# First tiles of a fused attention, MoE and MLP kernel: step 0's decays loaded as 8 rows, clipped there and spread over the partitions by products, C and x loaded straight into cleared blocks

## The chip, the cores and the metric

The kernel runs on one core of one Trainium2 chip. The metric is device time in microseconds (us), the median of several runs. Engines: PE is TensorE (PEld its weight loads), DVE VectorE, ACT ScalarE, POOL GpSimd, SP SyncE, whose queue issues most DMA transfers. PSUM is the memory that TensorE writes, SBUF the memory on which the other engines work, both of 128 partitions.

## The reference, cut to what matters

```python
# 1. chunked linear attention with decay: batch 4, heads 8, seq 768, head_dim 32, d_state 16
log_a = np.log(np.clip(a, 1e-06, 1.0))
...
    cum = np.cumsum(la, axis=-1)
    L = np.exp(cum[:, :, :, None] - cum[:, :, None, :]) * causal
    M = np.einsum('bhin,bhjn->bhij', Cc, Bc) * L
    y_intra = np.einsum('bhij,bhjd->bhid', M, xc)
    y_inter = np.einsum('bhin,bhnd->bhid', Cc, state) * np.exp(cum)[:, :, :, None]
    ...
    state = decay_full[:, :, None, None] * state + np.sum(Bx, axis=2)
# 2. top-1 MoE on the 3072 rows of 256: 8 experts, 256 -> 1024 -> 256
xn = x / (np.linalg.norm(x, axis=-1, keepdims=True) + 1e-06)
logits = xn @ en.T / tau
expert_idx = np.argmax(logits, axis=1)
    ...
    h = np.maximum(x[mask] @ w1[e], 0.0)
    out[mask] = gate_w[mask, None] * (h @ w2[e])
# 3. second MLP: 256 -> 2048 -> 256
h = x @ w_in
out = (h * np.cos(h)) @ w_out
```

The decays `a` are clipped to [1e-6, 1]. The products of decays that make up `L` are made here by a scan along a row, with no logarithm.

## The kernel before, in words

Three stages follow each other in one program: the attention with the router, the experts, the second MLP. The order of the instructions on each engine is the order in which the program emits them (`tc.manual_schedule()`). The first tiles of the attention are emitted after a list, the string `g.HEAD`; each of its words is a letter for an operation and a number (the dictionary `start`): `p` pre, `s` scores, `a` and `b` the two parts of `halves`, `y` mid, `e` a piece of `prep`, `i` pieces of `blocks`, `k` some products on zeros that only keep TensorE busy (`keep_warm`, tile `pw`), `l` step_1, `t` pieces of `constants`.

The attention goes in 6 steps t of 128 positions; a step has 4 tiles (t,b), one for each batch b. The partitions of a tile hold a pair (half of heads, position in a chunk of 64) or (head, d_state), so a decay row of one head has to stand on 64 or on 16 partitions. Of a tile these instructions matter here (lines of before):

- `pre`: the scan L171, `L <- ac, DD` on VectorE: `ac` are the decays, the same 2048 numbers on 64 partitions, with a zero at the start of each chunk, and `DD` is 1 where a new row begins; then `last` (L176, VectorE) and `bp <- bn, last` (L178, POOL).
- `scores`: `ps <- CB, BTb` (L189, PE). `CB` holds C in four blocks of partitions, zero elsewhere; `BTb` is B masked by ACT (L147).
- `halves`: `pu <- XB, bp` (L205, PE), `M <- ps, L` (L208, VectorE), the state `st` (L219, L221, VectorE). `XB` holds x in blocks, made by ACT (L152) from `xc`.
- `mid`: `py <- CP, st` (L234) and `py <- M, XB` (L239, both PE), `yT <- py` (L242, ACT).
- once in a step, `prep`: the scan `ee <- az, D` (L158) and four products `CP <- CB, ee` (L161), all VectorE. `az` are the decays again, on 16 partitions for each head.

For steps 1 to 5 the decays are clipped once, all together, as tiles `ao` (L402), stored to DRAM as `acd` and `azd` (L403), and loaded from there, one row on 64 or 16 partitions (`load_ac`, L77; `load_az`, L85). Step 1's loads are issued in `step_1`, behind the stores. Step 0's decays are loaded unclipped from the input with the same spreading transfer (`ac`, four pieces of 128 KB and two of 256 KB, and `azr`, 256 KB) and clipped on 128 partitions by VectorE (`clip_ac` L91, `clip_az` L96). Step 0's `CB` is made from `ct` by masked copies on VectorE (L485) and ACT (L483); the `XB` of steps 0 and 1 is made by ACT. From step 2 on, x is loaded straight into `XB`; C is so from step 1 on.

`experts` (three POOL instructions on `er`, L347 to L351) and `constants` prepare the router: `em` (L408, scaled embeddings, VectorE), its transposition `pe` (PE), `IE` (the identity beside it), `tri`, `acc`, `ident`.

Of the kernel before, what the change touches and what calls it, by code (L numbers as in the profile page):

```python
# [25 lines left out]
C_D, C_EI, C_M4, C_M2, C_ONE, C_ID, C_TRI, C_W = 0, 64, 72, 76, 80, 96, 224, 352  # L26


def consts():
# [12 lines left out]

def attn_router(ctx, tc, g):
# [34 lines left out]

    def load_az(t):
        az = sb2.tile([128, 520], F32, tag="az", name="az")  # L80
        if t == 0:
            T[0]["azr"] = sb2.tile([128, 8, 64], F32, tag="M", name="azr", bufs=3)
            nc.sync.dma_start(T[0]["azr"].rearrange("p c i -> p (c i)"), g.A2[t].unsqueeze(1).to_broadcast([8, 16, 512]))
        else:
            nc.sync.dma_start(az, g.azd[t].unsqueeze(1).to_broadcast([8, 16, 520]))  # L85
# [2 lines left out]
    def clip_ac(c0, c1):

        ac = T[0]["ac"][:, c0:c1]  # L90
        nc.vector.tensor_scalar(ac, ac, 1.0, 1e-6, op0=ALU.min, op1=ALU.max)  # L91
        nc.vector.memset(ac.rearrange("p (q i) -> p q i", i=64)[:, :, 0:1], 0.0)

    def clip_az():
        az = T[0]["az"].rearrange("p (c i) -> p c i", i=65)
        nc.vector.tensor_scalar(az[:, :, 1:], T[0]["azr"], 1.0, 1e-6, op0=ALU.min, op1=ALU.max)  # L96
        nc.vector.memset(az[:, :, 0:1], 0.0)
# [26 lines left out]
    def load_b3(t):  # L124
        if t:
            return
        ct = big.tile([128, 512], F32, name="ct")
        nc.sync.dma_start(ct, g.CT[t])
        T.setdefault(t, {}).update(ct=ct)

    def load_b(t):
# [35 lines left out]
    def pre(t, b):  # L167
# [310 lines left out]
    pre(*tiles[0])
    def masked_c(c0, c1, on_act):
        for p in range(4):  # L480
            o, i, m = CB[0][:, p, c0:c1], T[0]["ct"][:, c0:c1], cst[:, C_M4 + p:C_M4 + p + 1]
            if on_act:
                nc.scalar.activation(o, i, AF.Copy, scale=m)  # L483
            else:
                nc.vector.tensor_scalar(o, i, m, None, op0=ALU.mult)  # L485

    masked_c(0, 128, False)
# [1 line left out]
    for _ in range(4):
        next(first)  # L490
    masked_c(128, 256, False)
    for _ in experts_:
        pass
    first_prep = prep(0)

    def step_1(_):
        store_a()
        nc.sync.dma_start(cst[:, C_ID:], g.CST[:, C_ID:])
        loads = dict(n=lambda: load_b2(1), c=lambda: load_b3(1), a=lambda: load_ac(1, 0, 512), A=lambda: load_ac(1, 512), f=lambda: load_ac(1), z=lambda: load_az(1))
        for op in g.LD:  # L500
            loads[op]()
# [6 lines left out]
    def front_b(n):  # L508
        for _ in fronts[n]:
# [943 lines left out]
```

## Time and profile before

| | |
|---|---|
| median of 3 runs | 578.29 us (577.97 to 578.92) |
| profiled execution | 580.77 us |
| span of its trace, first to last instruction | 579.1 us |
| mean granted TensorE clock | 0.983 of full |
| busy: PE, DVE, ACT, POOL | 95%, 77%, 51%, 54% of the span |

The span is the time from the first to the last instruction of the profiled execution; 1.67 us of its time lie outside the span. All instruction times below come from that one execution.

### The profile page before, as it was taken

The numbers are of one execution on the slowest core, as the hardware profiler recorded it, in microseconds if no ns is written. First come the engines' busy times: TensorE is split into PE (matmuls) and PEld (weight loads), VectorE is DVE, ScalarE is ACT, GpSimd is POOL, SyncE is SP. The second block draws the span as 40 slices with busy tenths as digits, with TensorE's granted clock in tenths as the row PEclk, the third lists the DMA queues.
The fourth block names the chain that finished last, engine by engine and source line by source line (L and its number), as shares of the span: only waits on it lengthen the run. The fifth ranks groups of instructions, "written<-read, shape, count | busy, mean of one in ns | idle before, by whom it ended". The sixth has DMA issues, their size and how long they took to land.

```text
span 579.1 us, 11037 instructions
## 1 busy us (share of the span) xinstructions
PE 552.6 (95%) x4000; PEld 502.0 (87%) x4000; DVE 444.9 (77%) x878; ACT 298.0 (51%) x637; POOL 310.5 (54%) x343
## 2 busy tenths in 40 slices
PE   7899999999798999999999999999999999999994
PEld 5678887898687999998998999999999999999994
DVE  6899999866576998798849867777766777776882
ACT  5253533544356575666756545445445445445562
POOL 4323543462254666474655747746746745745763
PEclk8989999999888999999999999999999999999999
DMA  7999885137675676644210000100100100100000
GB/s 211 243 222 210 198 241 168 41 118 235 199 184 210 183 198 220 222 139 173 82 2 1 2 1 2 36 1 2 37 0 1 38 1 1 38 1 6 33 20 19
DMA packets 28993, 57.00 MB, mean 98 GB/s; under 512 B 7216, under 2 KB 16056, under 8 KB 28184
## 3 DMA queue, kind: packets, MB, share of 16 engines
q1 hardware_dynamic: 26184, 47.77, 29.3%
q0 software_dynamic: 2752, 8.51, 4.3%
q8 instruction: 32, 0.52, 0.4%
q14 instruction: 25, 0.20, 0.1%
HBM read 48.50 MB, written 11.07 MB: 103 GB/s over the span
## 4 chain that ended last, share of the span: by engine, by line
PE 57%; DVE 9%; DMA 4%; issue 2%; ACT 2%; POOL 1%; POOLq 0%; SPq 0%; ACTq 0%
PE po L1372 22%; PE pu L1338 22%; PE py L1204 6%; PE ph L1234 6%; DMA xg<-xs 4%; DVE hl L1239 2%; DVE ta L1090 2%; DVE xg L863 1%; POOL gl L1409 1%; DVE ta L1094 1%; ACT hh L1238 1%; DVE lg L844 1%; DVE lg L840 1%; DVE ta L1088 1%; DVE wof L1101 1%
## 5 line engine op out<-in xcount | busy, mean ns | idle before, releaser
L1409 POOL TENSOR_TENSOR gl<-gg,gh 128x512 fp32r<-128x512 f32 (+1 forms) x111 | 125.7, 1138 | 105.2 <-PE pu L1338 63.4
L1399 ACT ACTIVATE cc<-ff,half 128x512 f32<-128x512 f32 (+1 forms) x112 | 74.2, 663 | 128.9 <-DVE ff L1397 128.9
L1395 DVE TENSOR_SCALAR tt<-pu 128x512 f32<-128x512 f32 (+1 forms) x110 | 67.5, 613 | 64.4 <-PE pu L1338 64.2
L1372 PE MATMUL po<-h,gl 128*128 128x256 f32 x384 | 108.3, 282 | 0.0
L1372 PE MATMUL po<-l,gh 128*128 128x256 f32 x384 | 108.3, 282 | 0.0
L1372 PE MATMUL po<-h,gh 128*128 128x256 f32 x382 | 107.7, 282 | 0.0
L752 POOL TENSOR_TENSOR l<-r,h 128x512 fp32r<-128x512 f32 x50 | 69.5, 1406 | 48.7 <-ACT h L743 48.3
L1372 PEld LDWEIGHTS po<-h,gh 128*128 128x128 f32 x382 | 72.3, 189 | 3.6
L1372 PEld LDWEIGHTS po<-l,gh 128*128 128x128 f32 x384 | 72.6, 189 | 3.1
L1372 PEld LDWEIGHTS po<-h,gl 128*128 128x128 f32 x384 | 73.1, 190 | 0.1
L1397 DVE SCALAR_TENSOR_TENSOR ff<-tt,pu 128x512 f32<-128x512 f32 (+1 forms) x110 | 67.1, 610 | 3.8
L1338 PE MATMUL pu<-yh,il 128*128 128x512 f32 (+1 forms) x192 | 68.6, 357 | 0.0
L1338 PE MATMUL pu<-yh,ih 128*128 128x512 f32 (+1 forms) x192 | 68.3, 356 | 0.0
L1338 PE MATMUL pu<-yl,ih 128*128 128x512 f32 (+1 forms) x192 | 68.0, 354 | 0.0
L1405 DVE SCALAR_TENSOR_TENSOR gg<-pu,cc 128x512 f32<-128x512 f32 (+1 forms) x110 | 66.7, 606 | 0.7 <-ACT cc L1399 0.4
L1408 ACT CAST gh<-gg 128x512 fp32r<-128x512 f32 (+1 forms) x112 | 60.8, 543 | 0.7 <-DVE gg L1405 0.6
L1239 DVE SCALAR_TENSOR_TENSOR hl<-ph,hh 128x432 fp32r<-128x432 f32 (+1 forms) x64 | 36.6, 576 | 20.1 <-ACT hh L1238 20.1
L1204 PE MATMUL py<-hl,h 128*128 128x432 f32 (+1 forms) x128 | 46.5, 363 | 4.4 <-DVE hl L1239 4.3
L1238 ACT ACTIVATE hh<-ph 128x432 fp32r<-128x432 f32 (+1 forms) x64 | 32.9, 514 | 28.9 <-PE ph L1234 28.4
L1204 PE MATMUL py<-hh,h 128*128 128x432 f32 (+1 forms) x128 | 46.0, 359 | 1.8 <-ACT hh L1238 1.8
L1204 PE MATMUL py<-hh,l 128*128 128x432 f32 (+1 forms) x128 | 45.9, 359 | 0.0
L1234 PE MATMUL ph<-xl,h 128*128 128x432 f32 x112 | 41.0, 366 | 2.1 <-DVE xl L1057 2.1
(220 smaller groups left out, 1208.4 us busy)
## 6 DMA issues: line engine op xcount, KB each, us to landing
r<-in_w SPq DMA_DIRECT2D x32, 512.0 KB, 5.9
ac<-acd SPq DMA_DIRECT2D x10, 512.0 KB, 6.4
raw<-in_w_in SPq DMA_DIRECT2D x8, 512.0 KB, 6.0
raw<-in_w_out SPq DMA_DIRECT2D x8, 512.0 KB, 3.3
xg<-xs SPq DMA_DIRECT2D x7, 462.4 KB
xs<-zd SPq DMA_DIRECT2D x5, 462.4 KB
XB<-in_X SPq DMA_DIRECT2D x8, 256.0 KB
bt<-in_BT SPq DMA_DIRECT2D x6, 256.0 KB, 8.7
```

Source lines behind the costliest of these rows:

```text
L752: (nc.vector if engines[q] == "v" else nc.gpsimd).tensor_tensor(out=l[:, s], in0=W[e][rn][:, s], in1=h[:, s].bitcast(F32), op=ALU.subtract)
L1204: nc.tensor.matmul(py[m][:, :b_.shape[1]], lhsT=a_[:, q, 128 * m:128 * m + 128], rhs=b_, start=q == 0 and k == 0, stop=q == 7 and k == 2)
L1234: nc.tensor.matmul(ph[:, :n], lhsT=a_[:, c, 128 * f:128 * f + 128], rhs=b_[:, c], start=k == 0, stop=k == 5)
L1239: nc.vector.scalar_tensor_tensor(out=hl, in0=ph[:, :n], scalar=0.0, in1=hh.bitcast(F32), op0=ALU.max, op1=ALU.subtract)
L1338: nc.tensor.matmul(PU[u], lhsT=a_[:, c, 128 * f:128 * f + 128], rhs=b_[:, c], start=c == 0 and k == 0, stop=c == 1 and k == 2)
L1372: nc.tensor.matmul(po[:, i], lhsT=a_[:, s], rhs=b_, start=first and per == 1, stop=q == NF - 1 and k == 2 and i == per - 1)
L1395: nc.vector.tensor_scalar(tt, pu, 0.25, MAGIC, op0=ALU.add, op1=ALU.add)
L1397: nc.vector.scalar_tensor_tensor(out=ff, in0=tt, scalar=-MAGIC, in1=pu, op0=ALU.add, op1=ALU.subtract)
L1399: nc.scalar.activation(cc, ff, AF.Sin, bias=half, scale=-TWO_PI)
L1405: nc.vector.scalar_tensor_tensor(out=gg, in0=pu, scalar=TWO_PI, in1=cc, op0=ALU.mult, op1=ALU.mult)
L1408: nc.scalar.copy(gh, gg)
L1409: (nc.vector if u >= len(units) else nc.gpsimd).tensor_tensor(out=gl, in0=gg, in1=gh.bitcast(F32), op=ALU.subtract)
```

## The change

For step 0 the two inputs of decays are loaded as 8 rows of 512 numbers each (tile `rows`), clipped there by VectorE (`clip_first`, two instructions on 8 partitions), and spread over 128 partitions by f32 products on TensorE with a matrix of ones and zeros (`sel`, 20 KB more of the constants) into PSUM (`spread`): first b = 0 and `az` together, then b = 1 and 2, then b = 3. The scan of b = 0 reads its decays in PSUM; ACT copies the others to `ac` and `az`. The PSUM tile is of the tag `y`, of which there is one buffer, that of `py`. C of step 0 and x of step 1 are loaded straight into `CB[0]` and `XB[1]`, which POOL clears first; `CB[1]` is cleared by VectorE in place of POOL. `DD` and part of `IE` are copied by ACT; the clips of `ao`, the copies of `tri`, `acc` and the rest of `IE` go to POOL. The loads of `em` and `tau` go from POOL's queue to SP's, the square of `em` and `experts` into `constants`, and the words of `g.HEAD` are new.

```diff
+    def load_first():
+
+        T[0] = dict(ac=sb2.tile([128, 2048], F32, tag="ac", name="ac"), az=sb2.tile([128, 520], F32, tag="az", name="az"))
+        a1, a2 = T[0]["rows"] = [sb2.tile([128, 512], F32, tag="M", name="rows", bufs=3)[:8] for _ in range(2)]
+        nc.sync.dma_start(a1, g.A1[0].rearrange("h (b q) -> (h b) q", b=4))
+        nc.sync.dma_start(a2, g.A2[0])
+
+    def clip_first(k):
+        a = T[0]["rows"][k]
+        nc.vector.tensor_scalar(a, a, 1.0, 1e-6, op0=ALU.min, op1=ALU.max)
+        if k == 0:
+            nc.vector.memset(a.rearrange("p (q i) -> p q i", i=64)[:, :, 0:1], 0.0)
+
+    def spread(k):
+
+        o = psY.tile([128, 2, 512], F32, tag="y", name="spread")
+        a1, a2 = T[0]["rows"]
+        ac = T[0]["ac"]
+        for i, b in enumerate(((0, None), (1, 2), (3,))[k]):
+            sel_ = sel[:, :128] if b is None else sel[:, 128 + 128 * b:256 + 128 * b]
+            nc.tensor.matmul(o[:, i], lhsT=sel_, rhs=a2 if b is None else a1, start=True, stop=True)
+        for i, b in enumerate(((0, None), (1, 2), (3,))[k]):
+            if b is None:
+                az = T[0]["az"].rearrange("p (c i) -> p c i", i=65)
+                yield
+                nc.scalar.copy(az[:, :, 1:], o[:, i].rearrange("p (c i) -> p c i", i=64))
+            elif b:
+                nc.scalar.copy(ac[:, 512 * b:512 * b + 512], o[:, i])
+            else:
+                T[0]["ac0"] = o[:, i]
...
-        for p in range(4 if t else 0):
+        for p in range(4):
             nc.sync.dma_start(CB[s][32 * p:32 * p + 32, p], g.CT[t, 32 * p:32 * p + 32])
...
-        if t < 2:
-            xc = T[t]["xc"] = sb2.tile([128, 1024], F32, tag="xc", name="xc")
+        if t < 1:
+            xc = T[t]["xc"] = big.tile([128, 1024], F32, tag="xc", name="xc")
...
-    nc.gpsimd.dma_start(em, g.emb)
-    nc.gpsimd.dma_start(tau, g.tau.unsqueeze(0).to_broadcast([E, 1]))
+    nc.gpsimd.memset(CB[0], 0.0)
+    nc.gpsimd.memset(XB[1], 0.0)
+    nc.vector.memset(warm, 0.0)
...
-    load_az(0)
-    load_ac(0, 512, 1024)
-    load_ac(0, 1024, 2048)
-    nc.gpsimd.memset(CB[1], 0.0)
+    nc.sync.dma_start(em, g.emb)
+    nc.sync.dma_start(tau, g.tau.unsqueeze(0).to_broadcast([E, 1]))
+    nc.sync.dma_start(cst[:, C_ID:], g.CST[:, C_ID:C_W])
+    nc.vector.memset(CB[1], 0.0)
...
     def store_a():
         for k, dst in enumerate((g.acd_t, g.azd_t)):
-            nc.vector.tensor_scalar(ao[k][:, :, 1:], ai[k][:, :, 1 - k:], 1.0, 1e-6, op0=ALU.min, op1=ALU.max)
+            nc.gpsimd.tensor_scalar(ao[k][:, :, 1:], ai[k][:, :, 1 - k:], 1.0, 1e-6, op0=ALU.min, op1=ALU.max)
             nc.sync.dma_start(dst, ao[k])
 
     def constants():
 
+        nc.scalar.activation(e2, em, AF.Square, accum_out=en)
+        for _ in experts():
+            pass
+        yield
         nc.vector.reciprocal(tau, tau)
         nc.vector.tensor_scalar(em, em, er, tau, op0=ALU.mult, op1=ALU.mult)
...
+        nc.gpsimd.tensor_copy(IE[:, :, 0:128], cst[:, C_ID:C_ID + 128].unsqueeze(1).to_broadcast([128, 2, 128]))
+        yield
+        nc.scalar.copy(IE[:, :, 128:], pe)
...
-    g.WARM = 12
-    g.LD = "cnfz"
-    g.HEAD = "k2 l0 i1 a0 z0 m0 c1 k2 z1 s1 k3 b0 p1 k6 i1 s2 e0 c2 k2 k1 i9 a1 b1 y0 e0 p2 e0 e0 t1 k6 t1 t1 t1 t1"
+    g.WARM = 8
+    g.HEAD = "v0 c0 c1 d0 B0 k1 i2 B0 p0 s0 e0 i2 B1 s1 k3 i1 a0 p1 l0 e0 b0 B2 k1 i1 s2 a1 e0 b1 y0 p2 e0 e0 i2 t1 t1 t1 t1 t1 t1"
```

VectorE from its first copy to the first product M of step 0, before (a row is line, operation, out<-in, shape):

```order
L475 COPY DD<-cst 128x512
L91 TENSOR_SCALAR ac<-ac 128x512
L92 MEMSET ac 128x8
L171 SCALAR_TENSOR_TENSOR L<-ac,DD 128x512
L176 TENSOR_TENSOR last<-L,cst 128x16
L485 TENSOR_SCALAR CB<-ct,cst 128x128 x8
L402 TENSOR_SCALAR ao_130<-ai_132 128x3x63
L402 TENSOR_SCALAR ao_131<-ai_133 128x3x64
L208 TENSOR_TENSOR M<-ps,L 128x512
L96 TENSOR_SCALAR az<-azr 128x8x64
```

The same stretch of VectorE in the changed kernel (L184 is the scan, L171 that of `ee`, L221 is M):

```order
L391 MEMSET CB 128x2048
L515 MEMSET az 128x8
L98 TENSOR_SCALAR rows<-rows 8x512
L100 MEMSET rows 8x8
L98 TENSOR_SCALAR rows<-rows 8x512
L184 SCALAR_TENSOR_TENSOR L<-spread,DD 128x512
L189 TENSOR_TENSOR last<-L,cst 128x16
L171 SCALAR_TENSOR_TENSOR ee<-az,D_134 128x520
L221 TENSOR_TENSOR M<-ps,L 128x512
```

The copy of DD, the eight masked copies of C and the two wide clips of `ao` are gone from VectorE; the scan of the first tile stands behind a clear of `CB[1]` and two clips on 8 partitions. From the first scan of step 1 on, VectorE's rows are the same in both programs, in the same order.

ACT before, from the square of `em` to step 1's first block:

```order
L397 ACTIVATE e_200,en<-em 8x256
L147 ACTIVATE BTb<-bt,cst 128x64x2 x2
L147 ACTIVATE BTb<-bt,cst 128x64x6 x2
L152 ACTIVATE XB<-xc,cst 128x32x8 x2
L483 ACTIVATE CB<-ct,cst 128x256 x4
L152 ACTIVATE XB<-xc,cst 128x32x8 x6
L242 COPY yT<-py 128x2x2x64
L147 ACTIVATE BTb<-bt,cst 128x512 x2
```

ACT in the changed kernel, over the same stretch (L114 and L116 copy the spread decays, L165 makes `XB`, L419 is the square of `em`):

```order
L497 COPY DD<-cst 128x512
L160 ACTIVATE BTb<-bt,cst 128x64x2 x2
L114 COPY az<-spread 128x8x64
L160 ACTIVATE BTb<-bt,cst 128x64x6 x2
L116 COPY ac<-spread 128x512 x2
L165 ACTIVATE XB<-xc,cst 128x32x8 x2
L116 COPY ac<-spread 128x512
L165 ACTIVATE XB<-xc,cst 128x32x8 x2
L255 COPY yT<-py 128x2x2x64
L165 ACTIVATE XB<-xc,cst 128x32x8 x4
L419 ACTIVATE e_195,en<-em 8x256
L432 COPY IE<-pe 128x2x8
```

Before, the square of `em` was ACT's first piece of work and all of step 0's `XB` stood ahead of the first `yT`; now four copies of PSUM stand between the blocks, and the square stands behind the last `XB`.

POOL before, from its first `bp` to the fourth:

```order
L178 TENSOR_TENSOR bp<-bn,last 128x256
L347 TENSOR_TENSOR er<-en,pw 8x1
L349 TENSOR_SCALAR er<-er 8x1
L351 TENSOR_TENSOR er<-er,pw 8x1
L178 TENSOR_TENSOR bp<-bn,last 128x256 x2
L807 MEMSET zrow 108x1096
L810 DMA xs<-zrow 64x1096 x2
L178 TENSOR_TENSOR bp<-bn,last 128x256
```

POOL in the changed kernel, from the clips of `ao`, behind the second `bp`, to the fourth `bp` (L191 is `bp`, L360 to L364 `er`, L414 the clips of `ao`):

```order
L414 TENSOR_SCALAR ao_130<-ai_132 128x3x63
L414 TENSOR_SCALAR ao_131<-ai_133 128x3x64
L191 TENSOR_TENSOR bp<-bn,last 128x256
L360 TENSOR_TENSOR er<-en,pw 8x1
L362 TENSOR_SCALAR er<-er 8x1
L364 TENSOR_TENSOR er<-er,pw 8x1
L430 COPY IE<-cst 128x2x128
L434 CAST tri<-cst 128x128
L435 TENSOR_SCALAR acc_127<-cst 128x8
L808 MEMSET zrow 108x1096
L811 DMA xs<-zrow 64x1096 x2
L191 TENSOR_TENSOR bp<-bn,last 128x256
```

Before, `er` stood between the first and the second `bp`, and the clear of `zrow` right behind the third; now the clips of `ao`, on which the stores of the decays wait, stand between the second and the third `bp`, and `er`, the copies and the zeros between the third and the fourth.

## Rows read from the trace of the kernel before

**Rows 1.** The page's first part: busy time of the engines in us, share of the span, instructions.

```profile
PE 552.6 (95%) x4000; PEld 502.0 (87%) x4000; DVE 444.9 (77%) x878; ACT 298.0 (51%) x637; POOL 310.5 (54%) x343
```

**Rows 2.** Busy time in two stretches of the span: the stretch and its length, then PE, PEld, DVE, ACT, POOL busy us (instructions), granted clock, DMA share, GB/s.

```profile
32.00:108.00 76.00, 73.05 (x863) 61.21 (x864) 72.40 (x188) 32.45 (x104) 31.57 (x49) 0.98 0.75 192
...
200.00:579.00 379.00, 369.41 (x2337) 342.92 (x2336) 280.50 (x468) 203.12 (x387) 223.88 (x217) 1.00 0.16 50
```

**Rows 3.** VectorE's waits from 0 to 30 us: waiting instruction, what it waited for, us in total, times, longest.

```profile
DVE DD L475 <- DMA cst<-in_CST: 1.4, 1, 1.4
DVE ac L91 <- DMA ac<-in_A: 1.3, 2, 1.0
...
DVE L L171 <- DMA ac<-acd: 0.9, 1, 0.9
...
DVE az L96 <- DMA azr<-in_A: 0.7, 1, 0.7
```

**Rows 4.** Timeline of VectorE from the scaling of `em` to the second scan of step 1: start us, us, engine, line, operation, tiles; in brackets the idle time ahead and what ended it.

```profile
23.93 0.40 DVE L408 TENSOR_SCALAR em<-em,er,tau 8x256 f32<-8x256 f32 x1
...
25.09 1.15 DVE L171 TENSOR_TENSOR_SCAN L<-ac,DD 128x512 f32<-128x512 f32 x1
...
28.45 1.23 DVE L171 TENSOR_TENSOR_SCAN L<-ac,DD 128x512 f32<-128x512 f32 x1 [0.88 <-DMA ac<-acd]
...
30.24 1.67 DVE L171 TENSOR_TENSOR_SCAN L<-ac,DD 128x512 f32<-128x512 f32 x1 [0.28 <-issue]
```

**Rows 5.** Timeline of VectorE and POOL at the start.

```profile
1.03 0.27 DVE L378 MEMSET warm<- 128x256 uint32 x1
...
2.72 2.30 DVE L475 COPY DD<-cst 128x512 f32<-128x512 f32 x1 [1.40 <-DMA cst<-in_CST]
2.91 1.82 POOL L375 MEMSET CB<- 128x2048 f32 x1
...
6.02 0.43 DVE L91 TENSOR_SCALAR ac<-ac 128x512 f32<-128x512 f32 x1 [1.00 <-DMA ac<-in_A]
...
6.62 1.23 DVE L171 TENSOR_TENSOR_SCAN L<-ac,DD 128x512 f32<-128x512 f32 x1
```

**Rows 6.** TensorE's products in the timeline.

```profile
1.35 5.86 PE L384 MATMUL pw<-warm 128*128 128x272 bf16 x28 [1.35 <-DVE ao L394]
...
9.46 1.98 PE L189 MATMUL ps<-CB,BTb 128*128 128x256 f32 x4 [2.25 <-DVE CB L485]
...
14.06 2.25 PE L384 MATMUL pw<-warm 128*128 128x272 bf16 x18
...
16.14 1.22 PE L189 MATMUL ps<-CB,BTb 128*128 128x256 f32 x4
...
18.35 0.91 PE L205 MATMUL pu<-XB,bp 128*32 128x64 f32 x16 [0.29 <-POOL bp L178]
...
19.18 0.44 PE L234 MATMUL py<-CP,st 128*64 128x128 f32 x4
...
19.45 1.09 PE L239 MATMUL py<-M,XB 128*64 128x64 f32 x16
```

**Rows 7.** TensorE in three windows: the window and its length, PE busy us (instructions), granted clock, DMA share, GB/s.

```profile
10.00:11.00 1.00, 1.00 (x4) 0.50 1.01 274
14.00:15.00 1.00, 1.00 (x10) 1.00 1.04 164
22.00:24.50 2.50, 0.15 (x3) 1.00 1.01 223
```

**Rows 8.** ACT in the timeline, and from the list of groups by form one copy of PSUM later in the program (busy us, mean ns).

```profile
4.48 0.41 ACT L397 ACTIVATE e<-em 8x256 f32<-8x256 f32 x1 [2.12 <-DMA em<-in_emb]
...
4.81 0.18 ACT L397 ACTIVATION_READ_ACCUMULATOR e<-em 8x1 f32 x1
...
9.48 0.91 ACT L152 ACTIVATE XB<-xc,cst 128x256 f32<-128x256 f32 x2 [0.89 <-DMA xc<-in_X]
...
11.90 2.51 ACT L152 ACTIVATE XB<-xc,cst 128x256 f32<-128x256 f32 x6
...
20.59 0.37 ACT L242 COPY yT<-py 128x256 f32<-128x256 f32 x1 [6.18 <-PE py L239]
...
L1029 ACT COPY yd<-py 128x512 f32<-128x512 f32 x1 | 0.6, 592 | 0.0
```

**Rows 9.** POOL in the timeline: the first and the last of the three instructions on `er`, and two `bp`.

```profile
9.00 0.58 POOL L347 TENSOR_TENSOR er<-en,pw 8x1 f32<-8x1 f32 x1
...
10.22 0.57 POOL L351 TENSOR_TENSOR er<-er,pw 8x1 f32<-8x1 f32 x1
...
26.62 0.72 POOL L178 TENSOR_TENSOR bp<-bn,last 128x256 f32<-128x256 f32 x1 [0.92 <-DVE last L176]
...
30.10 0.73 POOL L178 TENSOR_TENSOR bp<-bn,last 128x256 f32<-128x256 f32 x1 [2.33 <-PE py L234]
```

**Rows 10.** SP's issues in the timeline, and the transfers of step 1's and step 2's decays (transfers, KB each, median us from issue to landing, from 0 to 32 us).

```profile
13.70 0.37 SPq L403 DMA_DIRECT2D acd<-ao  x1
...
18.10 1.10 SPq L77 DMA_DIRECT2D ac<-acd  x2
...
ac<-acd SPq DMA_DIRECT2D x4, 512.0 KB, 6.2
...
acd<-ao SPq DMA_DIRECT2D x1, 96.0 KB, 4.3
```

More of the change, by code (lines that the diff above doesn't have):

```diff
@@ L26 @@
 C_D, C_EI, C_M4, C_M2, C_ONE, C_ID, C_TRI, C_W = 0, 64, 72, 76, 80, 96, 224, 352
+C_SEL, C_ALL = 352, 992
 def consts():
-    c = np.zeros((128, C_W), np.float32)
+    c = np.zeros((128, C_ALL), np.float32)
     p = np.arange(128)
+    for k in range(8):
+        c[k, C_SEL:C_SEL + 128] = p // 16 == k
+        for b in range(4):
+            c[k, C_SEL + 128 + 128 * b:C_SEL + 256 + 128 * b] = (p // 64 == k // 4) * (k % 4 == b)
     c[:, C_ID:C_ID + 128] = np.eye(128)
@@ L70, in load_ac @@
     def load_ac(t, c0=0, c1=2048):
-        src = g.A1 if t == 0 else g.acd
+        src = g.acd
         if c0 == 0:
@@ L80, in load_az @@
         az = sb2.tile([128, 520], F32, tag="az", name="az")
[L81 to L85, printed above, removed]
-        T.setdefault(t, {})["az"] = az
[L88 to L97, printed above, removed]
+        nc.sync.dma_start(az, g.azd[t].unsqueeze(1).to_broadcast([8, 16, 520]))
+        T.setdefault(t, {})["az"] = az
+    def load_first():
[3 more added lines that the diff above has]
+        nc.sync.dma_start(a2, g.A2[0])
@@ L122, in load_b2 @@
             nc.sync.dma_start(XB[s][64 * h2:64 * h2 + 64, h2], g.X[t, 64 * h2:64 * h2 + 64])
[L124 to L129, printed above, removed]
     def load_b(t):
@@ L135, in load_b @@
         load_b2(t)
-        load_b3(t)
     def blocks(t):
@@ L148, in blocks @@
                 yield
-        for q in range(4 if t < 2 else 0):
+        for q in range(4 if t < 1 else 0):
             for h in range(2):
@@ L170, in pre @@
         L = sb2.tile([128, 2, 4, 64], F32, tag="L", name="L", bufs=4)
-        nc.vector.tensor_tensor_scan(out=L.rearrange("p c q i -> p (c q i)"), data0=T[t]["ac"][:, 512 * b:512 * b + 512], data1=DD,
+        nc.vector.tensor_tensor_scan(out=L.rearrange("p c q i -> p (c q i)"), data0=T[t]["ac"][:, 512 * b:512 * b + 512] if t or b else T[0]["ac0"], data1=DD,
                                      initial=0.0, op0=ALU.mult, op1=ALU.add)
@@ L360, in attn_router @@
     one = big.tile([128, 1], F32, name="one")
-    nc.gpsimd.memset(one, 1.0)
+    sel = big.tile([8, C_ALL - C_SEL], F32, name="sel")
+    warm = big.tile([128, 512], BF16, name="warm")
+    nc.gpsimd.memset(CB[0], 0.0)
+    nc.gpsimd.memset(XB[1], 0.0)
+    nc.vector.memset(warm, 0.0)
+    nc.vector.memset(one, 1.0)
     nc.scalar.activation(one, one, AF.Exp)
-    nc.gpsimd.dma_start(em, g.emb)
-    nc.gpsimd.dma_start(tau, g.tau.unsqueeze(0).to_broadcast([E, 1]))
+    load_first()
+    nc.sync.dma_start(sel, g.CST[:8, C_SEL:])
     nc.sync.dma_start(cst[:, :C_ID], g.CST[:, :C_ID])
-    load_ac(0, 0, 512)
     load_b1(0)
-    load_b3(0)
     load_b2(0)
@@ L413, in constants @@
         yield
-        nc.vector.tensor_copy(IE[:, :, 0:128], cst[:, C_ID:C_ID + 128].unsqueeze(1).to_broadcast([128, 2, 128]))
+        nc.gpsimd.tensor_copy(IE[:, :, 0:128], cst[:, C_ID:C_ID + 128].unsqueeze(1).to_broadcast([128, 2, 128]))
         yield
-        nc.vector.tensor_copy(IE[:, :, 128:], pe)
+        nc.scalar.copy(IE[:, :, 128:], pe)
         yield
-        nc.vector.tensor_copy(tri, cst[:, C_TRI:C_TRI + 128])
-        nc.vector.tensor_scalar(acc[0], cst[:, C_EI:C_EI + E], 8.0, SX / 128.0, op0=ALU.add, op1=ALU.mult)
+        nc.gpsimd.tensor_copy(tri, cst[:, C_TRI:C_TRI + 128])
+        nc.gpsimd.tensor_scalar(acc[0], cst[:, C_EI:C_EI + E], 8.0, SX / 128.0, op0=ALU.add, op1=ALU.mult)
         yield
@@ L474, in attn_router, with dd @@
     constants_ = constants()
-    nc.vector.tensor_copy(DD.rearrange("p (q i) -> p q i", i=64), cst[:, C_D:C_D + 64].unsqueeze(1).to_broadcast([128, 8, 64]))
-    clip_ac(0, 512)
     g.pull = lambda k: None
[L478 to L487, printed above, removed]
-    first = blocks(0)
[L489 to L493, printed above, removed]
+    first = blocks(0)
     first_prep = prep(0)
+    spreads = [spread(k) for k in range(3)]
+    def dd():
+        nc.scalar.copy(DD.rearrange("p (q i) -> p q i", i=64), cst[:, C_D:C_D + 64].unsqueeze(1).to_broadcast([128, 8, 64]))
     def step_1(_):
+        load_b2(1)
         store_a()
[L498 to L501, printed above, removed]
+        load_ac(1)
+        load_az(1)
     fronts = {}
@@ L512, in attn_router @@
     start = dict(a=front_a, b=front_b, s=lambda n: scores(*tiles[n]), p=lambda n: pre(*tiles[n]), y=lambda n: mid(*tiles[n]),
-                 c=lambda n: clip_ac(512 * n, 512 * n + (512 if n < 2 else 1024)), k=keep_warm, z=lambda n: (clip_az, lambda: next(first_prep))[n](),
-                 e=lambda n: next(first_prep), i=lambda n: [next(first, None) for _ in range(n)], m=lambda n: masked_c(256, 512, True), l=step_1, t=lambda n: [next(constants_, None) for _ in range(n)])
+                 c=clip_first, k=keep_warm, B=lambda n: next(spreads[n], None), d=lambda n: dd(), v=lambda n: nc.vector.memset(T[0]["az"].rearrange("p (c i) -> p c i", i=65)[:, :, 0:1], 0.0),
+                 e=lambda n: next(first_prep), i=lambda n: [next(first, None) for _ in range(n)], l=step_1, t=lambda n: [next(constants_, None) for _ in range(n)])
     for op in g.HEAD.split():
```

6 lines of the change are left out of this document (1 added, 5 removed).

## The prediction

> **What bounds the kernel now.** I read the page first. TensorE is busy for 95% of the span [rows 1], which invites the thought that nothing in the first 30 us can matter. The busy time by stretches corrects it: from 200 us on TensorE works 369.4 of 379 us, but from 32 to 108 us it is VectorE that fills its time, 72.40 of 76 us [rows 2], and the view of VectorE's waits has no entry in that stretch. TensorE's long part starts only when the attention's rows are scattered and gathered back, behind VectorE's last tile. So whatever moves VectorE's first instruction of the saturated stretch moves everything behind it, one for one. That instruction is the scan of tile (1,0): VectorE's order from there on is the same in both programs. It starts at 28.45 us, after 0.88 us of waiting for the load of step 1's decays; VectorE itself was free at 27.57 [rows 4]. The price of the change is where this scan starts afterwards.
>
> Ahead of it VectorE loses some 4 us to loads: 1.4 for the constants of DD, 1.3 for `ac`, 0.7 for `azr`, 0.9 for step 1's `ac` [rows 3].
>
> **The change, step by step.** In the changed program VectorE has far less to do before 28 us; what sets its scan is a chain through all the engines, which I sum in order.
>
> *Clips.* POOL's first two instructions are now two clears like the one of 1.82 us [rows 5], from about 1.5 to 5.1 us. VectorE clears `CB[1]` at the same time: eight times the bytes of the 0.27 us clear of `warm` [rows 5], 2.2 us as an estimate, 1.4 to 3.5. The rows have long landed by then (the first small load was usable at 2.72, the end of the wait in [rows 5]). But the copy of DD, normally a matter of the 0.43 us of the 128x512 clip, took 2.30 us and ended at 5.02, 0.29 behind POOL's clear, beside which it stood [rows 5]. So I let the first clip begin at 5.1 and take 0.6 with its memset (6.02 to 6.62, the start of the next row): the products begin at 5.75. If the clear did not hold it, it would be 5.0, when 16 warm-up products (28 took 5.86, so 3.4 from 1.35) [rows 6] leave TensorE free.
> The Trainium skill (SBUF — State Buffer, section "Who interferes with whom") says that VectorE's two-port operations and GpSimd's operations take the shared port pair for a whole instruction and the other blocks; the row agrees. By that rule the sum stays as it is; without it, it would be 0.7 us lower.
>
> *First spread pair.* The trace has no product of this shape. The nearest is `ps`, two products of 256 columns: 1.22 us with the clock at 1.00 and 1.98 at 0.50 [rows 6, 7]. The part that scales is 0.76 at full clock, so the fixed part is 0.46, and two products of 512 columns take 2 x 0.76 + 0.46 = 1.98 at full (3.5 at half), one 1.2. The early warm-ups ran mostly at the lower level (28 in 5.86 us, 0.21 each, against 18 in 2.25, 0.125 each, at 14 us [rows 6]), so I add 0.3: 5.75 to 8.05.
> *First scan.* It waits for ACT's copy of `az` as well, 0.59 for a 128x512 copy of PSUM [rows 8]: 8.7. Scan 1.23 [rows 5]: 10.0.
> *Second pair.* One buffer for `spread`, so it waits for that scan: 10.0 to 12.0; ACT's copy of b = 2 behind it to 12.65; ACT's first `XB` pair 0.91 [rows 8] to 13.55; `pu` of (0,0) 0.91 [rows 6] to 14.5.
> *Third.* Product b = 3 behind `pu`, 1.1: 15.6; copy 16.25; `XB` pair 17.15; `pu` of (0,1) 18.1; `py` (19.18 to 20.54, 1.36 [rows 6]) 19.45; `yT` 0.37 [rows 8] 19.87; the four blocks left at 0.42 each (2.51 for six [rows 8]) 21.55.
> *Router.* The square of `em` now stands behind all of this on ACT: 0.41 and the read of its sum to 4.99, 0.51 [rows 8], 22.1; the three `er` on POOL 1.79 (9.00 to 10.79 [rows 9]), 23.95. VectorE waits here with `em`, and the scan of (0,3), its `last`, M and `st` are queued behind. That is the new wait, some 2 us long. `em` takes 0.40 [rows 4]; POOL's copy into `IE` starts beside it and may hold it for up to 0.4, I add 0.2: the scan of (0,3) starts at 24.6 where it started at 25.09.
> *To (1,0).* From there to VectorE being free was 25.09 to 27.57, 2.48 us [rows 4], and the instructions are the same: **27.1 us against 28.45, 1.35 us earlier.**
>
> What is removed at no price of its own: the masked copies, wide clips and constants on VectorE, and eight `XB` copies of step 1 on ACT. VectorE waits at four places of this chain (the clip, two scans, `em`), so its own work is not what the chain is made of. The new clear of `CB[1]` is costed at nothing because POOL's two clears and the warm-up products last longer; alone it would be 2.2 us.
>
> **The load of step 1's decays.** It must be in by 27.1. Before, the store was issued at 13.70 and landed in 4.3 us, the loads were issued at 18.10, and the last was awaited until 28.45, 10.35 us later, although the median to landing was 6.2 [rows 4, 10]. Now the clips stand on POOL behind `bp` of (0,1), whose scan follows ACT's copy of b = 1: scan from about 12.7 to 13.9, `last` and `bp` to 15, the first clip at POOL's 0.5 to 0.8 to 15.6. The store is issued 2 us later. Against that, 1.25 MB of spreading transfers (four of 128 KB, two and one of 256 KB) are gone from a queue that was full (DMA share 1.01 to 1.04 [rows 7]); at its 164 to 274 GB/s they were some 4.6 to 7.6 us. So I take 2.5 for the store, loads issued at 18.3, and landing between the median, 24.5, and before's 28.5: around 26, just hidden.
>
> **Sum.** The profiled execution of 580.77 us would become 579.4; on the median of 578.29 that is **576.9 us**.
>
> Costs that the trace leaves open: POOL's fourth `bp` moves from beside M (0.72, no loss) to beside the scans of step 1, where the scan (1,1) took 1.67 instead of 1.23, with 0.28 idle ahead, next to `bp` [rows 4, 9]: 0 to 0.7 more, I take 0. The same loss may also vanish, -0.7. The lock on the first clip and on `em`: -0.9 to +0.2.
>
> **Rivals.**
> *A, the load stays the bound (no change).* Its row before speaks for it, 10.35 us in spite of the median; against it the lighter queue. With loads issued at 18.3 and before's 10.35 it lands at 28.65: 578.5 us, same.
> *B, TensorE at its lower level.* The clock stood at 0.50 from 10 to 11 us, after TensorE had idled for 2.25 us ahead of `ps`, and at 1.00 from 22 to 24.5, where it worked for 0.15 us [rows 6, 7]. Now the spread products run early behind fewer warm-ups, and TensorE has nothing from 19.5 to 24.5. The first pair at 1.2 GHz costs 1.2 us more, the second 1.5, the third 0.8; one of them leaves 578.1 to 578.4, same. Both pairs and the third make it slower by 2: 580.4.
> The Trainium skill (TensorE: Matmul & The Clock Gate, Part 1) calls the lower level the default that activity releases. That this program's first products ran slow agrees.
> *C, faster than forecast.* No lock at the clip (0.7) and no loss at (1,1) (0.7): 575.5 us. The copy of DD speaks against the first; nothing in before shows the second.
> *D, slower: the store's delay goes through to the scan.* If the store, issued at 15.6, still needs 4.3 us, and the loads behind it 10.35, they land at 30.25: 1.8 us later than before, 580.1 us. It decides from a landing at 29.6 on (28.45 + 1.16). For it speaks that step 1's `bn` and x, 0.75 MB that followed the store, now stand ahead of it in SP's queue; against it the 1.25 MB that are gone.
>
> **Chances.** A measurement tells 0.2%, 1.16 us, from no change, so faster means below 577.13, and the forecast lies only 0.25 below that. The forecast has 0.48, with its own range from the lock, the scale of the products and the fourth `bp`: 576.0 to 577.6, seven tenths of it on the faster side. C has 0.15, A 0.13, B 0.12 (a third of it slower), D 0.08, waits that I have not seen 0.04 (slower). Faster: 0.34 + 0.15, 0.50; same: 0.14 + 0.13 + 0.08, 0.34; slower: 0.04 + 0.08 + 0.04, 0.16. The range for 8 in 10 reaches from a little below C through A and B's milder cases and leaves D out: 575.2 to 578.9.
>
> **What will show it.** VectorE's list of waits should have the clips at about 5.1 with a long first clip, scans waiting for ACT, and one wait of 1 to 3 us of `em` for POOL's `er`. The scan of (1,0) should start at 27.1 (26.4 to 28.4) with no wait for `ac`. If it names `acd` as its releaser, A or D holds. A spread pair that takes over 3 us, or a granted clock of 0.5 in its window, is B. From there to the end the distances should be those of before. I am wrong if VectorE waits after the scan of (1,0) in a place where it did not wait, or if the end does not move with the scan.

## The result and the profile after

The changed kernel is slower: 583.64 us against 578.41 (medians of 6), a ratio of 1.0089 with the interval 1.0069 to 1.0109. Its profiled execution took 583.12 us with a span of 581.5 us. Two of the executions below were disturbed, the profiled one of er_early (860.34 us) and one of after_again (590.51 us); the recorded ratio of after_again, 1.0107, appears to count the latter, without which the ratio of the medians is 1.0092.

The first steps went as summed. In the timeline of the changed kernel (start us, us, engine, line, operation, tiles) the first clip, beside POOL's second clear (3.17 to 4.97), took 2.47 us, the products followed at 6.04 for 1.98 us, and the first scan began at 8.67. Then the second pair took 3.78 us:

```profile
3.38 2.47 DVE L98 TENSOR_SCALAR rows<-rows 8x512 f32<-8x512 f32 x1
...
5.90 0.40 DVE L98 TENSOR_SCALAR rows<-rows 8x512 f32<-8x512 f32 x1
...
6.04 1.98 PE L109 MATMUL spread<-rows,sel 8*128 8x512 f32 x4 [0.97 <-DVE rows L100]
...
8.67 1.22 DVE L184 TENSOR_TENSOR_SCAN L<-spread,DD 128x512 f32<-128x512 f32 x1 [2.36 <-ACT az L114]
...
10.11 3.78 PE L109 MATMUL spread<-rows,sel 8*128 8x512 f32 x4
...
13.81 2.10 PE L202 MATMUL ps<-CB,BTb 128*128 128x256 f32 x4
...
14.88 0.92 ACT L165 ACTIVATE XB<-xc,cst 128x256 f32<-128x256 f32 x2
...
15.71 1.56 PE L398 MATMUL pw<-warm 128*128 128x272 bf16 x6
...
17.20 0.89 PE L218 MATMUL pu<-XB,bp 128*32 128x64 f32 x16
...
27.18 0.46 DVE L424 TENSOR_SCALAR em<-em,er,tau 8x256 f32<-8x256 f32 x1 [1.55 <-POOL er L364]
...
29.95 1.21 DVE L184 TENSOR_TENSOR_SCAN L<-ac,DD 128x512 f32<-128x512 f32 x1
```

The windows of TensorE (length, busy us and instructions, granted clock, DMA share, GB/s) name the reason. The granted clock, 1.00 at the upper level of 2.4 GHz and 0.50 at the lower of 1.2 GHz, fell in the window from 8 to 10 us and stayed at 0.50 until 18, although TensorE worked without a gap; and it was there again at 27.7 to 31:

```profile
8.00:10.00 2.00, 2.00 (x7) 0.56 1.05 296
10.00:16.00 6.00, 6.00 (x11) 0.50 0.69 200
16.00:18.00 2.00, 2.00 (x22) 0.50 0.00 0
18.00:20.00 2.00, 2.00 (x10) 0.88 0.32 99
...
27.70:31.00 3.30, 3.26 (x40) 0.50 0.29 77
```

VectorE's waits of the first 30 us, which were loads in [rows 3], are now waits for engines:

```profile
DVE st L232 <- PE pu L218: 3.5, 2, 2.0
DVE L L184 <- ACT ac L116: 2.7, 1, 2.7
DVE L L184 <- ACT az L114: 2.4, 1, 2.4
DVE em L424 <- POOL er L364: 1.5, 1, 1.5
```

The scan of (1,0) starts at 29.95, where [rows 4] has 28.45 and the prediction 27.1. And a second loss follows, which the change of that one instruction does not hold: M of (0,3) starts 5.33 us after it (35.28), before 3.74, with this row of the kernel before behind those of [rows 4]:

```profile
32.19 0.69 DVE L208 TENSOR_TENSOR M<-ps,L 128x512 f32<-128x512 f32 x1
```

In the changed kernel POOL's work and VectorE's stand beside each other there:

```profile
30.51 1.41 POOL L811 DMA_DIRECT2D xs<-zrow  x2 [0.32 <-POOL zrow L808]
...
31.78 1.21 DVE L184 TENSOR_TENSOR_SCAN L<-ac,DD 128x512 f32<-128x512 f32 x1
31.93 1.57 POOL L191 TENSOR_TENSOR bp<-bn,last 128x256 f32<-128x256 f32 x1
...
33.54 0.45 DVE L189 TENSOR_TENSOR last<-L,cst 128x16 f32<-128x16 f32 x1 [0.55 <-POOL bp L191]
...
33.91 1.42 POOL L191 TENSOR_TENSOR bp<-bn,last 128x256 f32<-128x256 f32 x2
33.91 1.44 DVE L279 TENSOR_TENSOR lg<-yr 128x8 f32<-128x8 f32 x1
...
35.28 0.68 DVE L221 TENSOR_TENSOR M<-ps,L 128x512 f32<-128x512 f32 x1
```

The fourth `bp`, 26.62 in [rows 9], now comes at 31.93, behind `er`, the copies and the zeros; those of (1,0) and (1,1) queue behind it. A sum of 128x8 numbers, `lg`, takes 1.44 us where two `bp` start at the same moment (0.16 in the kernel before). From there on the distance to the kernel before stays: M of (0,3) 3.1 us later, POOL's transfer `xs <- zd` at the router's end 130.24 against 127.22, and in between VectorE's last scan, here before and after:

```profile
107.21 1.21 DVE L171 TENSOR_TENSOR_SCAN L<-ac,DD 128x512 f32<-128x512 f32 x1
...
110.19 1.21 DVE L184 TENSOR_TENSOR_SCAN L<-ac,DD 128x512 f32<-128x512 f32 x1
```

### The profile page after: what moved, and what is told of

Its sections match the earlier page's. It is cut to its first block, busy times and chain, and to the rows that moved or that the text cites. A ratio compares the mean times of both kernels' runs of the same rounds, so it can differ in the third digit from the quotient of the medians.

```text
span 581.5 us, 10953 instructions
## 1 busy us (share of the span) xinstructions
PE 553.4 (95%) x3968; PEld 498.7 (86%) x3968; DVE 442.2 (76%) x859; ACT 296.1 (51%) x631; POOL 314.8 (54%) x348
## 4 chain that ended last, share of the span: by engine, by line
PE 56%; DVE 8%; DMA 5%; issue 2%; POOL 2%; ACT 2%; POOLq 0%; SPq 0%; ACTq 0%; DVEq 0%
PE po L1373 22%; PE pu L1339 20%; PE ph L1235 7%; PE py L1205 7%; DMA xg<-xs 4%; POOL gl L1410 1%; DVE hl L1240 1%; DVE ta L1091 1%; DVE lg L845 1%; DMA pidf<-dense 1%; DMA r<-in_w 1%; DVE ta L1095 1%; DVE lg L841 1%; ACT hh L1239 1%; DVE wof L1102 1%
```

## The experiments

Ratios are to the kernel before on the same chip, in the same series. The first eight ran on one chip, the last four on another, on which the kernel before has a median of 582.02 us.

| kernel | median us | before | ratio (interval) | scan (1,0), us | M (0,3), us |
|---|---|---|---|---|---|
| pool_order | 580.31 | 578.33 | 1.0043 (1.0021 to 1.0064) | 31.21 | 34.44 |
| er_early | 580.37 | 578.33 | 1.0032 (1.0016 to 1.0048) | – | – |
| warm | 580.65 | 578.33 | 1.0038 (1.0019 to 1.0058) | 28.61 | 33.94 |
| k128 | 579.76 | 578.33 | 1.0015 (0.9996 to 1.0035) | 28.35 | 33.68 |
| after_again | 584.64 | 579.13 | 1.0107 (1.0065 to 1.0148) | 30.15 | 34.17 |
| before_again | 579.5 | 579.13 | one execution | 29.17 | 32.89 |
| combo | 578.72 | 579.13 | 0.9998 (0.9980 to 1.0016) | 30.22 | 33.60 |
| combo_warm | 577.43 | 579.13 | 0.9973 (0.9957 to 0.9989) | 26.40 | 29.60 |
| cold | 586.23 | 582.02 | 1.0080 (1.0053 to 1.0108) | 32.04 | 37.37 |
| after_third | 585.6 | 582.02 | one execution | 29.98 | 35.29 |
| before_pool | 583.14 | 582.02 | 1.0011 (0.9988 to 1.0035) | 29.74 | 33.74 |
| combo_store | 581.01 | 582.02 | 0.9968 (0.9943 to 0.9994) | 25.64 | 28.92 |

The last two columns, the marks, are start times in the trace of one execution each. From M of (0,3) to VectorE's last scan every one of these traces has 74.9 to 75.1 us, only combo 75.8, so a mark carries over to the end of VectorE's row. But behind the router's end (the first `xs <- zd`) they have anything from 446.8 to 451.9 us left, whichever the kernel; so the marks tell where, the medians how much. No marks are read from er_early.

**pool_order.**

```diff
-    g.ZN = {1: 3, 8: 1, 13: 1}
-    g.HEAD = "... i2 t1 t1 t1 t1 t1 t1"
+    g.ZN = {4: 3, 8: 1, 13: 1}
+    g.HEAD = "... i2 t1 t1 t1 t1 t1"
```

> The changed kernel with POOL's order alone altered: the clear of zrow and the two transfers of zeros, and the copies of tri, acc and ident, stand behind the fourth bp (that of tile (0,3)), as most of them did before the change. If the pile of POOL work ahead of that bp is what stretches VectorE's row from the scan of (1,0) at 29.95 to M of (0,3) at 35.28 (5.33 us against 3.74 before), this distance falls to 3.7 to 4.2 and the time by 1.1 to 1.6 us against the changed kernel's 583.6. If the stretch comes from TensorE at its lower level (28 to 32 us) instead, the distance stays above 5.

In its timeline the distance from the scan of (1,0) to M of (0,3) is 3.23 us:

```profile
31.21 1.22 DVE L184 TENSOR_TENSOR_SCAN L<-ac,DD 128x512 f32<-128x512 f32 x1
...
32.56 1.31 DVE L184 TENSOR_TENSOR_SCAN L<-ac,DD 128x512 f32<-128x512 f32 x1
...
34.44 0.68 DVE L221 TENSOR_TENSOR M<-ps,L 128x512 f32<-128x512 f32 x1
```

TensorE's clock stood at 0.50 at 28 to 33 us here too, so the order on POOL is the cause of the stretch, not the clock. The size was missed: the median lies 3.3 us below the changed kernel's, where 1.1 to 1.6 were expected, while M of (0,3) came only 0.8 us earlier in this trace, since its scan of (1,0) came 1.3 us later. What the rest of the gain is, no row shows.

**er_early.**

```diff
+    def early():
+        nc.scalar.activation(e2, em, AF.Square, accum_out=en)
+        for _ in experts():
+            pass
...
     def constants():
 
-        nc.scalar.activation(e2, em, AF.Square, accum_out=en)
-        for _ in experts():
-            pass
-        yield
...
-    g.HEAD = "... e0 i2 B1 ..."
+    g.HEAD = "... e0 i2 q0 B1 ..."
```

> The changed kernel with the square of em and the three er instructions moved to where ACT and POOL wait for the second spread pair (around 10 to 14 us); nothing else. Theory of the late router: VectorE's wait of 1.55 us ahead of em is gone and the scan of (1,0) starts 1.5 to 2 us earlier than 29.95, the time falls by 1.5 to 2. Rival: the load of step 1's decays (issued at 19.39) or POOL's pile takes the place of the wait, and the time falls by less than 0.7.

The time fell, by 3.3 us, more than the 1.55 us of the wait, though within the width of the intervals. That the wait is gone is seen in combo, which has the same edit: there `em` starts at 27.44 without a wait.

**warm.**

```diff
-    g.WARM = 8
-    g.HEAD = "... B0 p0 s0 e0 ..."
+    g.WARM = 11
+    g.HEAD = "... B0 p0 s0 k5 e0 ..."
```

> The changed kernel with 6 more warm-up products ahead of the first spread pair and 10 more behind ps of (0,0). Theory of the clock: the second spread pair took 3.78 us because TensorE stood at 0.50 from 8.4 to 18.2 us; with more other products around the spread products it stays at 1.00, the pair takes 2.0 and the chain up to pu of (0,1) gets 2.5 to 3.5 us shorter, less some 1 us that the products cost. Rival: the spread products of 8 rows themselves go with the lower level, whatever stands around them: the clock is at 0.50 around 11 to 14 us again, the pair takes 3.5 or more, and the time is that of the changed kernel or 1 us worse.

The second pair took 1.98 us (the first 2.08), and the scan of (1,0) came 1.3 us earlier than in the changed kernel, although the first products started 0.4 us later. The same 8-row products run at the upper level when other products stand around them. Behind the pair the lower level came all the same: the next six warm-up products took 1.57 us, as in the changed kernel.

```profile
6.46 2.08 PE L109 MATMUL spread<-rows,sel 8*128 8x512 f32 x4
11.01 1.98 PE L109 MATMUL spread<-rows,sel 8*128 8x512 f32 x4
```

**k128.**

```diff
-        a1, a2 = T[0]["rows"] = [sb2.tile([128, 512], F32, tag="M", name="rows", bufs=3)[:8] for _ in range(2)]
+        rows = [sb2.tile([128, 512], F32, tag="M", name="rows", bufs=3) for _ in range(2)]
+        T[0]["all"] = rows
+        for z in rows:
+            nc.vector.memset(z, 0.0)
+        a1, a2 = T[0]["rows"] = [z[:8] for z in rows]
...
-        a1, a2 = T[0]["rows"]
+        a1, a2 = T[0]["all"]
...
-    nc.sync.dma_start(sel, g.CST[:8, C_SEL:])
+    nc.sync.dma_start(sel, g.CST[:, C_SEL:])
```

> The changed kernel with the spread products on all 128 rows (the rows beyond 8 are zeros, cleared by two more VectorE memsets, and the matrix of ones is loaded with 128 rows). If the clock falls because TensorE's products have only 8 rows, it stays at 1.00 through the second pair, which takes 2.0 instead of 3.78, and the time falls by 2 to 3 us. If the rows do not matter, the clock reads 0.50 from 8.4 on again and the time is within 0.5 us of the changed kernel's.

The first pair, whose start behind the longer loads is the same, took 3.78 us, the second 1.98, and the clock's column reads 1.00 through both:

```profile
6.03 3.78 PE L113 MATMUL spread<-rows,sel 128*128 128x512 f32 x4 [0.86 <-DVE rows L104]
...
11.74 1.98 PE L113 MATMUL spread<-rows,sel 128*128 128x512 f32 x4 [0.27 <-DVE L L188]
```

So the second pair ran at the upper level behind a first pair at the lower one, and the time is some 4 us below the changed kernel's, more than the 2 to 3 expected. The nearest comparison is the trace of combo, which has the changed kernel's program up to the first pair. Its 16 warm-up products took 3.81 us as here and its first pair 3.78, but on 8 rows its second pair took 3.78 as well:

```profile
6.03 3.78 PE L109 MATMUL spread<-rows,sel 8*128 8x512 f32 x4 [0.86 <-DVE rows L100]
...
12.01 3.78 PE L109 MATMUL spread<-rows,sel 8*128 8x512 f32 x4
```

That speaks for the rows, with one trace on each side; warm shows that other products around 8-row ones are enough too. And the column cannot be read as the speed of the first products.

**after_again, after_third, before_again** are the two kernels unaltered.

> The changed kernel once more, unaltered, beside the variants and on the same chip. If its first trace is typical, the scan of (1,0) starts at about 30 us, M of (0,3) at about 35.3, and its time lies 4 to 6 us above the kernel before; if the lower clock of the first trace (0.50 from 8.4 to 18.2 us) was that execution's alone, the marks lie 1 to 3 us earlier and the difference is 2 to 3 us.

> The changed kernel for a third trace: if the clock's course in the first 20 us varies between executions, the second or the first spread pair has another duration than in the two traces so far (1.98 and 3.78 us); if not, the scan of (1,0) starts at 29.9 to 30.2 us again.

> The kernel before once more, for a second trace: the scan of (1,0) at 28.4 to 28.5 us and M of (0,3) at 32.2 us if its first 30 us are the same in every execution; its profiled execution of 580.77 us lay 2.4 above its median, so something behind 130 us should be some 2 us shorter here.

All three traces of the changed kernel have a first pair of about 2 us, a second of 3.78 and the scan of (1,0) at 29.95 to 30.15. The kernel before has it at 28.45 and 29.17, with the same 3.7 us to M. M of (0,3) is thus 1.3 to 3.1 us later in the traces of the changed kernel, but the medians differ by 5.2 and 5.3 (584.43 against 579.13). In after_again `lg` came just ahead of the two `bp`, took 0.15 us, and M followed 4.02 us after the scan instead of 5.33:

```profile
33.72 0.45 DVE L189 TENSOR_TENSOR last<-L,cst 128x16 f32<-128x16 f32 x1 [0.55 <-POOL bp L191]
34.09 0.15 DVE L279 TENSOR_TENSOR lg<-yr 128x8 f32<-128x8 f32 x1
34.17 0.68 DVE L221 TENSOR_TENSOR M<-ps,L 128x512 f32<-128x512 f32 x1
```

**cold.**

```diff
-    g.WARM = 8
+    g.WARM = 1
```

> The changed kernel with 2 warm-up products ahead of the first spread pair in place of 16. Theory of the clock: in many executions of the changed kernel TensorE is at the lower level from the start through both spread pairs, although the first traces show the first pair at full speed (1.98 us); then this kernel, whose first pair must take 3.5 us or more, has the same time as the changed kernel on its chips, 583.5 to 585, 5 to 6 us above the kernel before. Rival: most executions of the changed kernel are as its traces; then this one is 1.5 to 2.5 us slower than it, 7 to 8 us above the kernel before.

The ratio, 1.0080, is the changed kernel's (1.0089, and 1.0092 by the medians in after_again). Both pairs took 3.78 us:

```profile
6.03 3.78 PE L109 MATMUL spread<-rows,sel 8*128 8x512 f32 x4 [4.04 <-DVE rows L100]
...
12.01 3.78 PE L109 MATMUL spread<-rows,sel 8*128 8x512 f32 x4
```

while the column of the granted clock shows 1.00 in the same stretch, before its first change:

```profile
6.00:8.00 2.00, 1.97 (x3) 1.00 0.89 304
8.00:10.00 2.00, 2.00 (x5) 1.00 1.02 283
10.00:16.00 6.00, 6.00 (x11) 1.00 0.83 210
```

Its six executions read mean clocks of 0.980 to 0.989. Of eleven executions of the changed kernel (without the one of 590.51 us), four read 0.975 to 0.979 and took 581.3 to 583.1 us; seven read 0.985 or 0.986 and took 583.3 to 585.1. Its three traces read 0.974 to 0.979. So I take it that in two executions of three the changed kernel runs its first pair at the lower level too, which the column doesn't count, and is then some 2 us longer than in its traces: M of (0,3) at 37.4 as in cold, 4.8 us behind the kernel before. The trace of combo shows that this start can go either way: up to the first pair it is the same program, and there the pair took 3.78 us under a mean clock of 0.988. In pool_order, too, the executions that read 0.984 to 0.986 took some 2 us longer on average than those at 0.973 to 0.976; in combo the times do not split so. For the changed kernel itself it remains argued, as none of its traces shows it.

**before_pool.**

```diff
-    for _ in experts_:
-        pass
...
     def constants():
 
+        for _ in experts_:
+            pass
         nc.vector.reciprocal(tau, tau)
...
-        nc.vector.tensor_copy(IE[:, :, 0:128], ...
+        nc.gpsimd.tensor_copy(IE[:, :, 0:128], ...
...
-        nc.vector.tensor_copy(tri, cst[:, C_TRI:C_TRI + 128])
+        nc.gpsimd.tensor_copy(tri, cst[:, C_TRI:C_TRI + 128])
```

> The kernel before with one part of the change alone: er, the copies into IE, of tri and acc stand on POOL between the third and the fourth bp. Theory of the pile: the fourth bp starts at 28.5 us or later instead of 26.6, runs beside the scans of step 1, and M of (0,3) comes 5 us or more behind the scan of (1,0) instead of 3.74; the time grows by 1.0 to 1.6 us. Rival: the stretch in the changed kernel comes from TensorE's lower clock there; then the distance stays at 3.7 to 4.1 and the time is that of the kernel before.

A miss: the fourth `bp` did move to 29.92 and ran beside the scan of (1,0), but the distance to M is 4.00 us; `lg` took 0.15 us ahead of the last `bp`, as in after_again. The time isn't told apart from the kernel before. Distance and time are those that the rival of the clock gave; yet that rival does not hold, since the clock stood at 0.57 from 30 to 32 us here too, and pool_order had its 3.23 us while it stood at 0.50. So the pile costs 0.3 us when `lg` comes first, and 1.6 when two `bp` come first, as in two of three traces of the changed kernel and in warm, k128 and cold.

```profile
29.74 1.30 DVE L171 TENSOR_TENSOR_SCAN L<-ac,DD 128x512 f32<-128x512 f32 x1
29.92 1.64 POOL L178 TENSOR_TENSOR bp<-bn,last 128x256 f32<-128x256 f32 x1
...
33.74 0.68 DVE L208 TENSOR_TENSOR M<-ps,L 128x512 f32<-128x512 f32 x1
```

**combo, combo_warm, combo_store.** combo has the edits of pool_order and er_early, combo_warm those of warm as well, and combo_store one more:

```diff
-    g.HEAD = "... i1 a0 p1 l0 e0 ..."
+    g.HEAD = "... i1 l0 a0 p1 e0 ..."
```

> POOL's order as in pool_order and the early er as in er_early, both in the changed kernel. If the late router and the pile on POOL are two separate losses, they add: the scan of (1,0) starts 1.5 us earlier than in the changed kernel's own trace and M of (0,3) 3.2 to 3.7 us after it; the time is 2.5 to 3.5 us below the changed kernel's and within 1 us of the kernel before. If the lower clock alone makes the loss, the time stays 2 us or more above the kernel before.

> As combo, with the 6 and 10 more warm-up products of warm. If the lower clock is the third loss, the second spread pair takes 2.0 us, the scan of (1,0) starts at about 27 us, M of (0,3) at about 30.5, and the time is 1 to 2 us below combo's, the first variant below the kernel before. If not, the time is combo's plus up to 1 us.

> As combo_warm, with the clips of ao ahead of the second bp on POOL, so that the stores of the decays are issued some 2 us earlier. In combo_warm the scan of (1,0) waited 0.70 us for the load of step 1's decays; here it should not wait and start 0.5 to 0.7 us earlier, the time 0.4 to 0.7 us below combo_warm's 577.4. If the load is bound by the transfers ahead of it and not by the store, nothing changes.

combo has the time of the kernel before, though in its trace both pairs took 3.78 us: the late router and the pile are losses of their own. combo_warm is faster than both, 0.9973. Its timeline is the predicted chain, with the second pair at the upper level:

```profile
10.49 1.98 PE L109 MATMUL spread<-rows,sel 8*128 8x512 f32 x4
...
14.53 0.90 PE L218 MATMUL pu<-XB,bp 128*32 128x64 f32 x16
...
22.84 0.40 DVE L420 TENSOR_SCALAR em<-em,er,tau 8x256 f32<-8x256 f32 x1
...
26.40 1.23 DVE L184 TENSOR_TENSOR_SCAN L<-ac,DD 128x512 f32<-128x512 f32 x1 [0.70 <-DMA ac<-acd]
...
29.60 0.68 DVE L221 TENSOR_TENSOR M<-ps,L 128x512 f32<-128x512 f32 x1
```

Only here, with the chain short, does the load of step 1's decays come last, by 0.70 us. In combo_store that wait is gone and the scan starts at 25.64, M at 28.92; the times of the two aren't told apart.

## Why the prediction was wrong

**What bounds the kernel** was right: from M of (0,3) on, the changed kernel's rows keep their distance to those before until the router's end. But the price is not only the start of one scan: the row behind it was stretched by 1.6 us.

**Clips and first pair** were right in the three traces: products at 6.04 (5.75 predicted), 1.98 us, the first scan at 8.67 (8.7). The first clip was held as forecast, against rival C: it took 2.47 us beside POOL's clears, where the second, of the same shape, took 0.40. If the clock readings above are read rightly, the pair is at the lower level in most executions, 1.8 us where I had put 0.3.

**The second pair** is the step that failed. I took the upper level, 2.0 us; it took 3.78 in all three traces. Rival B had this term as 1.5 us more, measured 1.8, with too small a chance, 0.12 for the whole. The row that I set against it, 1.00 at 22 to 24.5 us in [rows 7], was no evidence for the first 15 us: there [rows 6] shows the level of the warm-up products only by their durations.

**`pu` of (0,0)** came at 17.20, 3.6 us later than the 13.6 of the sum. The pair makes up 1.8 of it. Behind it I had left out that `ps` of (0,1) and six warm-up products stand ahead of `pu` in TensorE's order: the `XB` pair was done at 15.80. At the upper level the omission costs less: 14.53 in combo_warm, 1.0 late, of which 0.5 lies in the later start of its second pair (10.49).

**The router** was right in kind: VectorE waited 1.55 us for `er`, 2 predicted; from `em` to the scan of (1,0) the distance is 2.8 us, 3.1 predicted.

**POOL's fourth `bp`**: 0 to 0.7, I took 0. Measured 1.6 in most traces and 0.3 in one. What I missed is that not one but three `bp` queue up, and that a short sum of VectorE is stretched beside two of them. The sign that I had named for being wrong, a new wait of VectorE behind the scan of (1,0), is there too: `last` waits 0.55 us for `bp`.

**The load of step 1's decays** did not bind. The store was issued at 17.73, 2.1 us later than predicted, but nothing was left in its way. The windows of the changed kernel (here with PE, PEld, DVE, ACT and POOL ahead of the clock) show an almost empty DMA from 15 to 18 us, then the store and the loads, and an empty one again ahead of the scan at 29.95:

```profile
15.00:18.00 3.00, 3.00 (x25) 1.59 (x23) 1.64 (x3) 0.80 (x2) 1.77 (x3) 0.50 0.04 11
18.00:28.00 10.00, 5.18 (x50) 3.69 (x46) 6.14 (x13) 3.75 (x10) 3.47 (x7) 0.84 0.63 153
28.00:30.00 2.00, 2.00 (x33) 1.69 (x34) 1.93 (x6) 1.42 (x3) 1.89 (x3) 0.50 0.00 0
```

Rivals A and D fall with it; the load ended last only in combo_warm, 8.4 us after its issue there (17.96 to 26.40). By that, an estimate, it was in at 27.8 in the changed kernel, where it was issued at 19.39.

**The rule on the shared port pair** goes further than the sentence cited for the clip: the Trainium skill (SBUF — State Buffer, "Who interferes with whom") also has a VectorE instruction with two inputs in SBUF contend with a GpSimd one that reads SBUF. Rows here agree: `tri`'s copy on POOL took 1.42 us beside a scan in the changed kernel and 0.28 in combo_warm, where none stood beside it.

The sum of the parts: the lower level and what stood ahead of `pu`, the late `er`, the pile. In the trace they make M of (0,3) 3.1 us later than before, where the sum had 1.35 us earlier; the other 2 of the 5.2 us between the medians are put down to the first pair, which is argued and not seen. Taken away together, the parts turn 1.0092 into 0.9973 on one chip. How much each is worth alone is less sure: pool_order, er_early and warm each lie 3 us below the changed kernel with intervals of some 2 us each, while the traces say 2.1 (the distance to M), 1.55 (the wait for `er`, read in the changed kernel) and 1.3 (the scan of (1,0)); and the three gains alone add up to 9.6 us, where combo_warm, with all three, gains 7.

## What to carry to other kernels

Work that is moved off the bounding engine to an idle one is free only if one reads what stands behind it in that engine's order, and what the bounding engine waits for from there: here a 0.15 us sum paid 1.3 us for POOL's queue. Give new products that stand on a chain both speeds of TensorE, and forecast the upper one only where a trace shows it for such a stretch. A sum over engines has to list all that stands in each queue ahead of each link, warm-up products too.

## What the runs showed of the hardware

TensorE stood at 1.2 GHz for some 10 us (0.56 in the window from 8 to 10, 0.88 in that from 18 to 20) while it worked without a gap on products of 8 rows, `ps` and few warm-up products; with 6 more of these ahead and 10 more between (1.98 us in warm), or with products of 128 rows (1.98 us in k128), the second pair ran at 2.4 GHz. In these traces the granted clock reads 1.00 until its first recorded change, whatever the speed: in cold, combo and k128 products of 3.78 us stand under 1.00, where 1.98 is the upper level's time. So in the first 20 us the durations decide, and a higher mean clock can belong to the slower execution.
